# Scores of a two-head attention as one float32 product of raw queries and keys, in place of three float32r products of their parts

## The chip, the cores and the metric

The kernel runs on one core of a Trainium2 chip. The metric is the device time of one execution in microseconds (us); the time of a kernel is the median of its runs.

## What is computed

The change is in the first of three stages. For 4 batches and 8 heads, with 576 positions and 64 values per head, all float32:

```
scores = 1/sqrt(D) * q @ k.T, causal, softmax -> a
local  = a @ v
phi(x) = where(x > 0, x, exp(x) - 1) + 1
mem    = (phi(q) @ M_prev) / (phi(q) . z_prev + 1e-6)
attn   = g * mem + (1 - g) * local          with g = sigmoid(beta)
x      = attn, heads side by side           (2304 tokens x 512)
x      = (h - tanh(h)) @ w_out              with h = x @ w_in        (512 -> 2048 -> 512)
out    = rational(h2) @ w2_out              with h2 = x @ w2_in      (512 -> 2048 -> 512)
```

## The kernel before

**Attention.** Heads are taken in pairs: 16 pairs n, both heads of one side by side on the 128 partitions, 64 rows each. A pair has five units i (`units`, `NU` = 5). Units 0 to 3 are 128 queries against 128, 256, 384 and 512 keys, one matmul group per head; unit 4 takes the last 64 queries of both heads together, with queries of the other head as zeros, against 512 keys and then the last 64.

The work is a pipeline over steps s, one unit entering per step (`step`, L576, with `ORDER` and `LAGS`): scores at once; the exponentials (`numer`) a step later; `scale` two steps later on GpSimd (POOL); `transposes` at lag 3, copied from PSUM by ScalarE (L491, L502); `values` at lag 4; `leave`, VectorE's copy out of PSUM (L818), at lag 5. While the first four pairs run, `values` has one PSUM bank, so the matmuls of a pair's last unit (L535) wait for VectorE's copy of the first four (L818).

**Parts.** `high` (L345) casts q and k to float32r (L351, ScalarE) and `low` (L355) subtracts that from the raw values (L361, VectorE for q, POOL for k), so each is the sum of two float32r parts, q1 + q2 and k1 + k2. `scores` (L413) then makes three products for each head into the same bank, q1 k1 + q1 k2 + q2 k1 (L432 to L438), and VectorE reduces them with the mask (L444).

**phi.** `phi1` to `phi3` (L366, L370, L374), `norm1` on POOL (L380, a product of phi and z), `norm2` on VectorE (L389 reduces that product), `norm3` on POOL (L397). `phiT` (L401) transposes on TensorE (L407), and VectorE copies both results (L410); `memory` (L509) multiplies them with M_prev in float32.

**Order.** The list `prep` (L304) says at which step, relative to the pair's first, each of these is issued, and `late` (L556) shifts some for the first two pairs. `load_k(n)` and `load_q(n)` issue five transfers for pair n + 1 on SyncE's (SP's) queue, at five and four steps before pair n's first unit, since pair n's casts have then been issued; the same queue carries the other inputs, weight loads (`wraw`) and stores (`wk`). Each step also advances a background (`tick`, L249): weights of the MoE are decoded (L164 on ScalarE, L166 to L174 on VectorE) and split (L184 on ScalarE, L186 on POOL), from step 10 on. When the first batch is done, at step 24, the first MoE's items for finished tokens are mixed in (`fill`, L913; L630 and L677 on TensorE), two items in a pair.

**After attention** come the rest of the first MoE and the second one, bound to TensorE and VectorE; none of their code is touched.

Of the kernel before, what the change touches and what calls it, by code (L numbers as in the profile page):

```python
# [9 lines left out]
F32 = mybir.dt.float32  # L10
F32R = mybir.dt.float32r
# [3 lines left out]
ALU = mybir.AluOpType  # L15
# [3 lines left out]
P = 128  # L19
# [41 lines left out]
def kernel(  # L61
# [21 lines left out]
    nc = tc.nc  # L83
    B, NP, _, _, S = qd.shape
# [14 lines left out]
    class Banks:  # L99
        def __init__(self, ids):  # L100
            self.ids, self.n = ids, 0
# [55 lines left out]
    def w_decode(layer, f, s):  # L157


        words = wraw.pop((layer, f, s)).bitcast(U32).rearrange("p (c t) -> p c t", t=2)  # L160
        low, high = words[:, :, 0], words[:, :, 1]
        x = bg.buf("wf", [P, DM], U32, f"wf{layer}_{f}_{s}")
        xf = x.bitcast(F32)
        nc.scalar.activation(xf, high.bitcast(F32), AF.Abs)  # L164
        yield
        nc.vector.tensor_scalar(xf, xf, E_MIN, E_MAX, ALU.max, ALU.min)  # L166
        nc.vector.tensor_scalar(
            x, x, 5, 2, ALU.logical_shift_left, ALU.logical_shift_right
        )
        yield  # L170
        nc.vector.scalar_tensor_tensor(
            x, high, 0xC0000000, x, ALU.bitwise_and, ALU.bitwise_or
        )
        nc.vector.scalar_tensor_tensor(  # L174
            x, low, 29, x, ALU.logical_shift_right, ALU.bitwise_or
        )
        yield
        return xf
# [113 lines left out]
    class Attention:  # L292
# [4 lines left out]
        def __init__(self, x_put, cp, sp, bS, bT, bV):  # L297
            self.x_put, self.cp, self.sp, self.bS, self.bT, self.bV = x_put, cp, sp, bS, bT, bV
            self.NU = NQ + 1
            self.units = [(n, i) for n in range(B * NP) for i in range(self.NU)]  # L300
            self.pair = [{} for _ in range(B * NP)]
            self.u = {}
            self.done = 0
            self.prep = [  # L304
                (-5, self.high, "k"), (-5, self.load_k, None), (-4, self.low, "k"),
                (-4, self.high, "q"), (-4, self.load_q, None), (-3, self.low, "q"),
                (-1, self.phi1, None), (0, self.phi2, None), (1, self.phi3, None),
                (2, self.norm1, None), (2, self.norm2, None), (3, self.norm3, None),
            ]
# [31 lines left out]
        def load_v(self, n):  # L341
            self.load("vn", n, [P, NQ + 1, P], vn, 2)


        def high(self, n, c, eng=None):  # L345

            d = self.pair[n]
            src = d["r" + c]
            d[c + "1"] = self.sp.tile([P, src.shape[1]], F32R, tag=c + "1", name=f"{c}1_{n}")
            if eng is None:  # L350
                nc.scalar.copy(d[c + "1"], src)  # L351
            else:
                eng.tensor_copy(d[c + "1"], src)

        def low(self, n, c, eng=None):  # L355

            d = self.pair[n]
            src = d["r" + c]
            d[c + "2"] = self.sp.tile([P, src.shape[1]], F32R, tag=c + "2", name=f"{c}2_{n}")
            eng = eng or (nc.gpsimd if c == "k" else nc.vector)  # L360
            eng.tensor_tensor(d[c + "2"], src, d[c + "1"].bitcast(F32), ALU.subtract)  # L361

        def phi1(self, n, _):
            d = self.pair[n]
# [36 lines left out]
        def phiT(self, n):  # L401
            d = self.pair[n]
            t = d["phiT"] = self.sp.tile([P, S], F32, tag="phiT", name=f"phiT{n}")
            for j0, j1, w in ((0, NQ, TB), (NQ, NQ + 1, TAIL)):
                ps = self.bT(f"php{n}_{j0}")
                for j in range(j0, j1):
                    nc.tensor.transpose(  # L407
                        ps[:, (j - j0) * P:(j - j0 + 1) * P], d["phi"][:, j, :], self.cp["ident"]
                    )
                nc.vector.tensor_copy(t[:, j0 * P:j0 * P + w], ps[:, 0:w])  # L410


        def scores(self, n, i):  # L413


            d, cp = self.pair[n], self.cp
            u = n * self.NU + i
            sm = cp["sm"][u % len(cp["sm"])]
            pts = []
            if i < NQ:  # L420
                w = (i + 1) * P
                jobs = [
                    (e, 0, w, slice(e * D, (e + 1) * D), cp["mask"][:, TB - i * P:TB + P])
                    for e in range(2)
                ]
                c0 = (i + 1) * P
            else:
                every = slice(0, P)
                jobs = [(0, 0, TB, every, cp["mask"][:, 0:TB]), (1, TB, S, every, cp["mask4"])]
                c0 = 0  # L430
            ps = [self.bS(f"s{n}_{i}_{c}") for c in range(2)]
            parts = (("q1", "k1"), ("q1", "k2"), ("q2", "k1"))  # L432
            for j, (q, k) in enumerate(parts):
                for c, k0, k1, r, _ in jobs:
                    nc.tensor.matmul(  # L435
                        ps[c][:, 0:k1 - k0], d[q][r, c0:c0 + P], d[k][r, k0:k1],
                        start=(j == 0), stop=(j == len(parts) - 1),
                    )  # L438
            for c, k0, k1, _, mask in jobs:
                if i < NQ or c == 0:  # L440
                    pts.append(self.sp.tile(
                        [P, k1 if i < NQ else S], F32, tag=f"p{i}_{c}", name=f"p{n}_{i}_{c}", bufs=1
                    ))
                nc.vector.tensor_tensor_reduce(  # L444
                    out=pts[-1][:, k0:k1], in0=ps[c][:, 0:k1 - k0], in1=mask, scale=-0.125,
                    scalar=3.0e38, op0=ALU.add, op1=ALU.min, accum_out=sm[:, 4 + c:5 + c],
                )
            if i == NQ:
                nc.vector.tensor_tensor(sm[:, 4:5], sm[:, 4:5], sm[:, 5:6], ALU.min)
            self.u[n, i] = {"p": pts, "sm": sm}  # L450
# [105 lines left out]
        def late(self, m, f, r):  # L556

            if m == 0:
                return r + (f in (self.phi3, self.norm1, self.norm2, self.norm3))
            return r + (m == 1 and r < 0 and f not in (self.load_q, self.load_k, self.phi1))  # L560

        def start(self, setup, setup2):

            self.load_k(-1)
            setup()
            self.load_n(0)
            self.high(0, "k")
            self.high(0, "q", nc.vector)
            self.low(0, "q")
            self.low(0, "k")  # L570
            self.load_k(0)
            self.load_q(0)
            setup2()
            self.phi1(0, None)

# [264 lines left out]
    def setup():  # L840
        for t in cp["rq"]:
            nc.vector.memset(t[0:D, TAIL:P], 0.0)
            nc.vector.memset(t[D:P, 0:TAIL], 0.0)
        attn.load_q(-1)
        nc.sync.dma_start(cp["g"], beta.partition_broadcast(P))
        nc.gpsimd.memset(cp["mask"], 0.0)
        nc.gpsimd.affine_select(
            out=cp["mask"][:, TB:TB + P], in_=cp["mask"][:, TB:TB + P],
            compare_op=ALU.is_ge, fill=NEG, base=0, pattern=[[-1, P]],
            channel_multiplier=1,  # L850
        )
        make_identity(nc, cp["ident"])
        for e in range(2):
            r = slice(e * TAIL, (e + 1) * TAIL)
            nc.vector.tensor_copy(cp["mask4"][r], cp["mask"][0:TAIL, TB:TB + TAIL])
        for sm in cp["sm"]:
            nc.vector.memset(sm, 1e-9)
        for pz in cp["pz"]:
            nc.vector.memset(pz[:, :, :, D:D + 1], 1e-6)

    def setup2():
        g, omg = cp["g"], cp["omg"]
        nc.scalar.activation(g, g, AF.Exp, scale=-1.0)
        nc.vector.tensor_scalar(g, g, 1.0, None, ALU.add)
        nc.vector.reciprocal(g, g)
        nc.vector.tensor_scalar(omg, g, -1.0, 1.0, ALU.mult, ALU.add)
        o2 = omg.rearrange("r (p e) -> r p e", e=2)
        for e in range(2):
            r = slice(e * TAIL, (e + 1) * TAIL)
            nc.vector.tensor_copy(cp["omg4"][r], o2[r, :, e])  # L870
# [112 lines left out]
    for s in range(ni + 2):  # L983
        if s < ni:
            t, f = items[s]
# [110 lines left out]
```

## Time and profile before

| | us |
|---|---|
| three runs | 1072.7, 1073.43, 1076.6 (median 1073.43) |
| the profiled execution, its own time | 1075.69 |
| its span, first to last instruction | 1073.9 |
| mean granted TensorE clock | 0.983 |
| busy: TensorE matmul / weight load | 1035.9 / 923.4 |
| busy: VectorE (DVE) / ScalarE (ACT) / GpSimd (POOL) | 876.2 / 689.7 / 439.8 |

Durations are taken from the profiled execution. TensorE's matmuls are pipelined: a record's duration holds its latency, and the distance of starts tells the cost of one in a sequence. Below, a line such as `PE pw L535` is an engine, the tile that is written and the line of the kernel. A wait in brackets is the engine's idle time before the instruction and what ended it.

### The profile page before, as it was taken

How to read it: one execution, taken by the hardware profiler on the slowest of the kernel's cores; microseconds unless marked ns; L12 is line 12 of the kernel's file. 1: busy time of each engine (PE TensorE's matmuls, PEld its weight loads, DVE VectorE, ACT ScalarE, POOL GpSimd, SP SyncE). 2: the span in 40 equal slices, each digit the busy share in tenths (PEclk: the TensorE clock that was granted, in tenths of full speed). 3: DMA queues.
4: the chain of work that ended last, by engine and by line, in shares of the span. 5: the costliest groups of instructions: out<-in, count | busy, mean ns of one | idle time of the engine just before them, and what ended most of it. 6: DMA issues, size and time to landing. Idle time of an engine off the chain costs nothing.

```text
span 1073.9 us, 18786 instructions
## 1 busy us (share of the span) xinstructions
PE 1035.9 (96%) x6704; PEld 923.4 (86%) x6704; DVE 876.2 (82%) x1786; ACT 689.7 (64%) x1507; POOL 439.8 (41%) x407
## 2 busy tenths in 40 slices
PE   6988999999999999999999998989999999999998
PEld 4656778878788999999999998878988989889886
DVE  6899988888767856767675755999999999999997
ACT  5866767768656453333333446878778887787875
POOL 6788877768725210101010103653333423434232
PEclk8987999999999999999999999999999999999999
DMA  5452342424142334444444341100000000000000
GB/s 161 127 163 90 118 133 81 161 81 138 43 130 78 108 108 116 120 127 138 119 118 129 116 137 54 46 1 21 10 1 31 1 20 11 1 30 1 20 11 30
DMA packets 35150, 84.07 MB, mean 78 GB/s; under 512 B 5872, under 2 KB 7920, under 8 KB 35056
## 3 DMA queue, kind: packets, MB, share of 16 engines
q1 hardware_dynamic: 35056, 82.86, 25.1%
q8 instruction: 53, 0.87, 0.3%
q14 instruction: 41, 0.34, 0.1%
HBM read 66.59 MB, written 16.25 MB: 77 GB/s over the span
## 4 chain that ended last, share of the span: by engine, by line
PE 56%; DVE 29%; ACT 8%; issue 4%; DMA 1%; SPq 1%; POOL 0%; POOLq 0%; ACTq 0%; DVEq 0%
PE h L630 20%; PE y L677 17%; DVE vA L741 9%; DVE vA L739 4%; PE s L435 4%; DVE vA L731 4%; PE tp L487 4%; PE y L763 4%; ACT vC L729 4%; ACT vC L730 4%; PE pv L521 3%; DVE vG L737 2%; DVE g L737 2%; PE pw L535 1%; DVE p L444 1%
## 5 line engine op out<-in xcount | busy, mean ns | idle before, releaser
L630 PE MATMUL h<-xs,w 128*128 128x384 f32 (+1 forms) x2448 | 440.1, 328 | 8.9 <-DVE g L745 3.2
L630 PEld LDWEIGHTS h<-xs,w 128*128 128x128 f32 x2448 | 408.1, 189 | 22.7 <-POOL xs L622 4.8
L677 PE MATMUL y<-gh,w 128*128 128x384 f32 (+1 forms) x864 | 216.5, 318 | 0.2 <-ACT gh L665 0.2
L763 PE MATMUL y<-w,gh 128*128 128x512 f32 x576 | 180.8, 395 | 0.2 <-ACT gh L750 0.2
L677 PEld LDWEIGHTS y<-gh,w 128*128 128x128 f32 x864 | 151.6, 188 | 1.3 <-ACT gh L665 0.6
L471 POOL TENSOR_SCALAR p<-p,sm,omg 128x128 f32<-128x128 f32 (+2 forms) x144 | 129.2, 904 | 53.8 <-DVE sm L465 20.1
L622 POOL TENSOR_TENSOR xs<-x,xs 128x256 fp32r<-128x256 f32 (+1 forms) x56 | 49.1, 899 | 232.3 <-ACT xs L621 224.8
L677 PE MATMUL y<-gl,w 128*128 128x384 f32 (+1 forms) x432 | 137.2, 318 | 1.2 <-DVE gl L666 0.9
L659 ACT ACTIVATE g<-h 128x384 f32<-128x384 f32 (+1 forms) x108 | 49.5, 458 | 118.4 <-PE h L630 117.5
L660 DVE TENSOR_TENSOR g<-h,g 128x384 f32<-128x384 f32 (+1 forms) x108 | 55.0, 510 | 86.2 <-ACT g L659 86.1
L763 PEld LDWEIGHTS y<-w,gh 128*128 128x128 f32 x576 | 106.6, 188 | 19.7 <-ACT o L771 1.7
L741 DVE TENSOR_TENSOR vA<-vA,vC 128x384 f32<-128x384 f32 x96 | 120.5, 1255 | 0.0
L763 PE MATMUL y<-w,gl 128*128 128x512 f32 x288 | 114.3, 397 | 1.0 <-POOL gl L752 1.0
L752 POOL TENSOR_TENSOR gl<-g,gh 128x384 fp32r<-128x384 f32 x48 | 57.9, 1207 | 136.7 <-ACT gh L750 114.8
L729 ACT ACTIVATE vC<-vA,coef 128x384 f32<-128x384 f32 x96 | 59.2, 617 | 78.5 <-DVE vA L741 78.5
L752 POOL TENSOR_TENSOR gl<-vG,gh 128x384 fp32r<-128x384 f32 x47 | 58.5, 1245 | 118.1 <-ACT gh L750 101.7
L491 ACT COPY pT<-tp 128x512 f32<-128x512 f32 (+2 forms) x112 | 55.6, 524 | 65.4 <-PE tp L487 64.8
L457 ACT ACTIVATE p<-p,sm 128x128 f32<-128x128 f32 (+2 forms) x144 | 83.5, 587 | 14.9 <-DVE sm L444 8.2
L665 ACT CAST gh<-g 128x384 fp32r<-128x384 f32 (+1 forms) x108 | 51.8, 480 | 57.5 <-PE y L677 56.4
L666 DVE TENSOR_TENSOR gl<-g,gh 128x384 fp32r<-128x384 f32 (+1 forms) x108 | 62.7, 581 | 27.5 <-ACT gh L665 27.5
L677 PEld LDWEIGHTS y<-gl,w 128*128 128x128 f32 x432 | 81.1, 188 | 2.1 <-DVE gl L666 2.1
L435 PE MATMUL s<-k,q 64*128 64x128 f32 (+4 forms) x480 | 72.9, 369 | 9.1 <-ACT k L351 6.5
(96 smaller groups left out, 1745.4 us busy)
## 6 DMA issues: line engine op xcount, KB each, us to landing
wraw<-in_w_in_dram SPq DMA_DIRECT2D x32, 512.0 KB, 4.1
wraw<-in_w_out_dram SPq DMA_DIRECT2D x32, 512.0 KB, 4.0
wk<-wf SPq DMA_DIRECT2D x44, 256.0 KB, 4.4
wx<-wk SPq DMA_DIRECT2D x22, 512.0 KB, 3.3
qn<-in_qn_dram SPq DMA_DIRECT2D x16, 320.0 KB, 4.0
vn<-in_vn_dram SPq DMA_DIRECT2D x16, 320.0 KB, 5.4
rk<-in_kd_dram SPq DMA_DIRECT2D x32, 144.0 KB, 5.2
out_dram<-o SPq DMA_DIRECT2D x18, 256.0 KB, 2.0
```

The lines of the kernel that those rows point to most:

```text
L435: nc.tensor.matmul(ps[c][:, 0:k1 - k0], d[q][r, c0:c0 + P], d[k][r, k0:k1], start=(j == 0), stop=(j == len(parts) - 1),)
L457: nc.scalar.activation(pt, pt, AF.Exp, bias=sm[:, 4 + e:5 + e], scale=-1.0, accum_out=sm[:, 2 * e:2 * e + 1],)
L471: nc.gpsimd.tensor_scalar(pt, pt, v["sm"][:, 6 + e:7 + e], og[:, c:c + 1], ALU.mult, ALU.mult)
L491: nc.scalar.copy(t[:, 0:w, :].rearrange("r t c -> r (t c)"), ps[:, 0:w * P])
L630: nc.tensor.matmul(ps[:, 0:T], wi_of(layer, f, wp, k), xs[k][:, xp], start=(n == 0), stop=(n == 3 * NK - 1),)
L660: nc.vector.tensor_tensor(v["g"], v["h"], v["g"], ALU.subtract)
L666: self.lo.tensor_tensor(v["gl"], v["g"], v["gh"].bitcast(F32), ALU.subtract)
L677: nc.tensor.matmul(ps, wo_of(1, f, w)[:, m * P:(m + 1) * P], v[g], start=(first and j == 0 and m % n == 0), stop=(last and j == 2), skip_g ...
L729: nc.scalar.activation(C, A, AF.Ln, bias=qeps_s, scale=TWO_M60)
L741: nc.vector.tensor_tensor(n["A"], n["A"], n["C"], ALU.mult)
L752: eng.tensor_tensor(o["gl"], o["G"], o["gh"].bitcast(F32), ALU.subtract)
L763: nc.tensor.matmul(acc_of[t][m], g[:, c], wo_of(2, f, w), start=(first and j == 0), stop=(last and j == 2),)
```

## The change

The parts are gone: no `high`, no `low`. `scores` issues for each head one product of the raw float32 tiles; for units 0 to 3 the two heads' products follow each other on different rows of the array, 64 rows each, in two PSUM banks. The loads of the next pair's q and k are issued at the pair's first unit, without the special cases in `late` and `start`. The two copies of phi's transposes go from VectorE to ScalarE.

```diff
             self.prep = [
-                (-5, self.high, "k"), (-5, self.load_k, None), (-4, self.low, "k"),
-                (-4, self.high, "q"), (-4, self.load_q, None), (-3, self.low, "q"),
+                (0, self.load_k, None), (0, self.load_q, None),
                 (-1, self.phi1, None), (0, self.phi2, None), (1, self.phi3, None),
...
-        def high(self, n, c, eng=None):
...
-        def low(self, n, c, eng=None):
...
-                nc.vector.tensor_copy(t[:, j0 * P:j0 * P + w], ps[:, 0:w])
+                nc.scalar.copy(t[:, j0 * P:j0 * P + w], ps[:, 0:w])
...
-            parts = (("q1", "k1"), ("q1", "k2"), ("q2", "k1"))
-            for j, (q, k) in enumerate(parts):
-                for c, k0, k1, r, _ in jobs:
-                    nc.tensor.matmul(
-                        ps[c][:, 0:k1 - k0], d[q][r, c0:c0 + P], d[k][r, k0:k1],
-                        start=(j == 0), stop=(j == len(parts) - 1),
-                    )
+            for c, k0, k1, r, _ in jobs:
+                nc.tensor.matmul(
+                    ps[c][:, 0:k1 - k0], d["rq"][r, c0:c0 + P], d["rk"][r, k0:k1],
+                    start=True, stop=True,
+                )
...
-            return r + (m == 1 and r < 0 and f not in (self.load_q, self.load_k, self.phi1))
+            return r
...
             self.load_n(0)
-            self.high(0, "k")
-            self.high(0, "q", nc.vector)
-            self.low(0, "q")
-            self.low(0, "k")
-            self.load_k(0)
-            self.load_q(0)
             setup2()
```

## Rows read from the trace of the kernel before

**Rows 1.** Stages: stretch, length, busy time of PE, PEld, DVE, ACT, POOL, clock, DMA.

```profile
0.00:32.09 32.09, 21.44 (x133) 14.51 (x134) 22.25 (x82) 17.49 (x47) 20.80 (x28) 0.84 0.49 145
32.09:45.13 13.04, 12.79 (x131) 9.16 (x132) 10.55 (x42) 11.04 (x31) 10.89 (x13) 1.00 0.65 200
45.13:62.23 17.10, 13.19 (x132) 9.18 (x132) 16.69 (x50) 12.79 (x34) 14.58 (x14) 0.95 0.46 142
62.23:81.74 19.51, 16.47 (x132) 12.17 (x132) 17.76 (x50) 12.81 (x33) 15.70 (x15) 0.76 0.41 124
81.74:103.30 21.56, 19.10 (x144) 13.88 (x144) 19.46 (x50) 14.30 (x38) 18.63 (x19) 0.78 0.37 112
103.30:124.36 21.06, 20.44 (x180) 16.49 (x180) 19.38 (x54) 13.46 (x35) 16.83 (x16) 0.92 0.36 116
124.36:301.67 177.31, 175.24 (x1706) 139.44 (x1705) 143.10 (x464) 126.27 (x351) 129.19 (x133) 1.00 0.32 102
301.67:1074.00 772.33, 757.20 (x4152) 708.55 (x4152) 627.01 (x1001) 481.52 (x939) 213.20 (x175) 1.00 0.21 63
```

**Rows 2.** Chain of waits, 235 to 262 us: start, length, engine, tile, line.

```profile
236.49 1.15 PE s L435 x6
...
239.88 0.48 PE s L435 x6
...
243.71 0.55 PE s L435 x6
...
246.08 0.72 PE s L435 x6
...
251.76 1.01 PE pv L509 x4
252.77 0.89 PE s L435 x6
...
255.02 1.15 PE s L435 x6
```

**Rows 3.** Timeline of VectorE, 29 to 71 us: start, length, instruction, idle before it.

```profile
29.32 0.83 DVE L361 TENSOR_TENSOR q<-rq,q 128x640 fp32r<-128x640 f32 x1
...
58.93 1.36 DVE L361 TENSOR_TENSOR q<-rq,q 128x640 fp32r<-128x640 f32 x1
60.21 0.82 DVE L389 TENSOR_REDUCE nrm<-pz 128x10 f32<-128x650 f32 x1
...
70.75 0.82 DVE L410 COPY phiT<-php 128x512 f32<-128x512 f32 x2 [0.66 <-PE php L407]
```

**Rows 4.** Timelines of POOL and of TensorE, 52 to 63 us.

```profile
52.70 1.58 POOL L361 TENSOR_TENSOR k<-rk,k 128x576 fp32r<-128x576 f32 x1
...
58.05 1.55 POOL L380 TENSOR_TENSOR pz<-phi,mz 128x640 f32<-128x640 f32 x1
...
62.23 1.53 PE L535 MATMUL pw<-pT,vn 128*64 128x64 f32 x20 [3.47 <-DVE x L818]
```

**Rows 5.** Stages, L361 alone: stretch, length, busy time of DVE, of POOL, clock.

```profile
62.23:81.74 19.51, 1.36 (x1) 1.43 (x1) 0.76 0.41 124
81.74:103.30 21.56, 1.80 (x1) 1.99 (x1) 0.78 0.37 112
```

**Rows 6.** Stages, L351 alone: stretch, length, busy time of ACT, clock.

```profile
45.13:62.23 17.10, 1.44 (x2) 0.95 0.46 142
```

**Rows 7.** Groups by shape, 32 to 302 us: instruction, count, busy, mean ns, idle.

```profile
L491 ACT COPY pT<-tp 128x512 f32<-128x512 f32 x60 | 33.6, 586 | 18.9 <-PE tp L487 18.9
...
L502 ACT COPY pT<-tq 128x64 f32<-128x64 f32 x15 | 3.3, 221 | 0.0
```

**Rows 8.** DMA issues of the whole span: tile, queue, count, size, us to landing.

```profile
rk<-in_kd_dram SPq DMA_DIRECT2D x32, 144.0 KB, 5.2
```

**Rows 9.** Timeline of ScalarE, 0 to 9 us.

```profile
4.42 1.28 ACT L351 ACT_TABLE_LOAD   x1 [4.42 <-DMA rk<-in_kd_dram]
...
7.21 0.21 ACT L863 ACTIVATE gg<-gg 128x8 f32<-128x8 f32 x1 [0.83 <-DMA gg<-in_beta_dram]
```

More of the change, by code (lines that the diff above doesn't have):

```diff
@@ L342, in load_v @@
             self.load("vn", n, [P, NQ + 1, P], vn, 2)
-        def high(self, n, c, eng=None):
[L347 to L353, printed above, removed]
-        def low(self, n, c, eng=None):
[L357 to L361, printed above, removed]
         def phi1(self, n, _):
```

## The prediction

> **What bounds the kernel now.** I read the stage table first: it cuts the span at the matmuls of L535, which close a pair of heads (the last unit's values). The reader sees three regimes [rows 1]. Up to 124.36 us a pair takes 13.0 to 21.6 us and VectorE is the fullest engine of most stretches: 16.69 of 17.10 us, 17.76 of 19.51, 19.46 of 21.56. From 124.36 to 301.67 TensorE is busy 175.24 of 177.31 us. After that come the two MoEs, which the change does not touch; I carry those 772.33 us over unchanged.
>
> Then the chain of waits in the middle regime: every link is TensorE, one after another, and the same unit of two successive pairs starts at 236.49 and at 255.02, so a pair costs 18.53 us of TensorE [rows 2]. The five score groups of one pair, in order of units 0 to 4, are 0.48, 0.55, 0.72, 0.89 and 1.15 us, 3.79 together. Here the change is paid for.
>
> Last the timelines of the first regime. Just before L535 VectorE does q's low part (58.93), the reduction of norm2 (60.21) and the copy that L535 waits for, while TensorE stands 3.47 us; POOL's product for that reduction starts only at 58.05, behind its own subtract at 52.70 [rows 3, 4]. The granted clock's mean is 0.76 and 0.78 in the fourth and fifth pairs against 1.00 in the second [rows 1]: mixtures of full clock (2.4 GHz) and half (1.2 GHz), in stretches that begin after such idle. Here the change earns.
>
> **Scores on TensorE.** Removed: three float32r products for each head; added: one float32 product. Of a float32 product this trace has L509 (two heads side by side, 512 columns): the program writes two per pair, the trace holds four records, so each product is two passes. The group takes 1.01 us [rows 2]. At 2.4 GHz two passes over 512 columns are 0.43 us at one cycle per column and 0.85 at two; I read it as two, which leaves 0.16 us of start and drain and the heads at the same time. By that, units 0 to 3 (128, 256, 384, 512 columns) cost 0.37, 0.59, 0.80, 1.01. Unit 4 is not split by rows: 576 columns, 0.96 us of passes plus 0.3 of the 0.43 that it now spends beyond its streaming, 1.26. Sum 4.03 against 3.79; the scores' weights are 128 columns wide where L509's are 64, so I take +0.30 per pair. Ends: +0.1 (no more overhead than L509) and +0.8 (all 1.47 us of today's overhead stays on top of 3.09 us of passes); I stay by L509, the same type and column count. The middle regime holds about 9.2 pairs of scores (177.31 / 18.53, less the last units' drain): **+2.8 us**, ends +1 and +7.
>
> **The parts.** Per pair this removes VectorE's q subtract (1.36 in the third and fourth pairs, 1.80 in the fifth), POOL's k subtract (1.43 to 1.99) and ScalarE's two casts (1.44) [rows 3 to 6]. Only the first two lie before something that ends late.
>
> **phi's copies.** VectorE loses 0.82 us per pair and the wait of 0.66 for the transposes in front of it [rows 3]. ScalarE takes two copies from PSUM, priced by its own copies of 512 and 64 columns: 0.59 + 0.22 = 0.81 [rows 7]. It lost 1.44, and is busy 12.8 of 17.1 or more [rows 1], so I cost this at nothing. The new wait on the transposes stands on ScalarE; queued behind it are phi2's exp, a weight cast and the next unit's exp, all used a step or more later. If that cover were gone it would cost 0.66 plus 0.81 per pair.
>
> **Loads.** The same five transfers per pair, issued five steps later for k and four for q, so past the inputs, weight loads and stores of a whole pair on SP. The casts stood five steps behind the transfers, the scores now do: 13 us or more, against a landing of 5.2 us [rows 1, 8]. Nothing. The buffer's last reader is now a score group of the step before; what queues behind that wait of SP's is the step's weight loads, used a tick later or more. For the second pair three other transfers go in front at the start, with 13 us to spare.
>
> **Sum over stretches** [rows 1]. *Start to 32.09:* the q subtract of the second pair goes, and the first scores need no parts. Against it, ScalarE's table load (1.28) stood until k landed at 4.42; its first work will be the gate's exp of L863, released at 7.21 [rows 9], and VectorE's next work hangs on that. From -2.5 to +0.5; I take -1.0. *Second pair (13.04):* TensorE 12.79 busy, so 0. *Third (17.10):* 1.36 + 0.82, and 0.4 for POOL's subtract being gone: VectorE's own took 0.83 at 29.32 and 1.36 at 58.93 beside a POOL instruction [rows 3, 4], so POOL's 1.58 may hold up another one by about that 0.53; ends 0 and 0.8. Less 0.3 for scores: -2.3 (-1.3 to -3.0). *Fourth (19.51):* 1.36 + 0.82 + 0.66 + 0.4: -3.2 (-1.5 to -4.1; VectorE's 16.3 covers the dearer scores). *Fifth (21.56):* the same with 1.80 for the subtract: -3.7 (-2 to -4.8). *Sixth (21.06):* down to the TensorE floor of 18.53 + 0.30, a little above for clock: -2.0 (0 to -2.3). Together -12.2; with +2.8 the net is **-9.4 us**. Other floors: TensorE at full clock needs 13.3 us for an unfilled pair, POOL 14.58 - 1.58 = 13.0 in the third, so VectorE's 14.5 still ends last. The profiled execution is 1075.69 us (span 1073.9), which gives 1066.3; it lies 2.3 us above the median 1073.43, so the forecast is 1064.0.
>
> **A rule weighed.** q's subtract took 0.83 at 29.32, and 1.36 at 58.93, where it ended 0.68 after POOL's product of 58.05 did (59.60) [rows 3, 4]. The Trainium skill (SBUF — State Buffer, Who interferes with whom) says that a VectorE instruction with two SBUF inputs and a GpSimd one that reads SBUF exclude each other for the whole instruction, the later one waiting; the two durations agree. By that rule 0.68 of the 1.36 is POOL's time, not the subtract's, and the sum over three stretches would be about 2 us smaller.
>
> **Rivals.** *(B) The reduction waits for POOL instead.* It reads the product that ends at 59.60, so without q's subtract it starts 0.61 earlier, not 1.36, unless POOL moves up. For it: that POOL item queues behind scales that need VectorE's and ScalarE's results. Against: POOL itself loses 1.58 just before. Then 0.61 + 0.82 in each of three stretches, -4.3; the clock still falls, so -1.2 in the sixth; start 0, scores +4: -1.5, 1072. *(C) The heads do not run side by side in float32 at 64 rows by 128 columns.* No row has this shape in this type; L509 splits columns as well. For against: float32r does it here, a 512-column group of six taking 0.89 [rows 2]. Price: the second head's passes, 2.13 us per pair, in series. Middle regime 9.2 x 2.4 = +22, second pair +2.4, sixth 0, the rest half of its gain, -5.5: +19, **1092**. It turns the sign once the extra exceeds about 1 us per pair. *(D) The clock stays full* as the 3.47 us idle shrinks, and the port relief is whole: most of the low ends, -15.5, with scores at +1: 1059. *(E) The change does not do what it says* and runs one float32r product each: some 2 us less per pair, -18 beside -12: 1043.
>
> **Chances.** A measurement here tells 0.5% (5.4 us) from no change. Forecast 0.54 (1060 to 1068), D 0.11, B 0.23, C 0.10, E 0.02. Faster 0.54 + 0.11 + 0.02 = 0.67; same 0.23; slower 0.10. The range leaves out C, E and the edge of D: 1058 to 1074.5.
>
> **What would show it.** Right: L361, L351 and L410 on VectorE gone, 320 records on the score line where there are 480, score groups in the middle regime of about 0.37, 0.6, 0.8, 1.0 and 1.25, a pair there of 18.8, and the matmuls of L535 of the sixth pair near 112 us instead of 124.36. Wrong: a 512-column group near 1.9 us (C); VectorE idle before the norm2 reduction with POOL as releaser (B); a pair of the middle regime above 19.3, or ScalarE busy without pause around phi's copies with TensorE waiting for them.

## The result, and the profile after

The kernel after takes 1063.97 us (median of four runs, 1061.86 to 1066.53), the kernel before 1073.74 (four runs): a ratio of 0.9907, 95% interval 0.9881 to 0.9934. The forecast was 1064.0. The profiled execution took 1061.86 us with a span of 1060.1.

The stage table of the kernel after, cut as before at the first matmul that closes a pair (now L514), with the same columns; its seven lines answer to the first seven of [rows 1]:

```profile
0.00:28.02 28.02, 19.49 (x116) 11.27 (x116) 16.52 (x76) 15.13 (x44) 15.55 (x25) 1.00 0.50 145
28.02:41.37 13.35, 13.22 (x122) 8.26 (x121) 8.94 (x39) 10.41 (x30) 8.82 (x11) 1.00 0.59 196
41.37:56.34 14.97, 13.32 (x123) 8.32 (x122) 13.90 (x47) 12.48 (x34) 11.77 (x12) 1.00 0.51 159
56.34:71.82 15.48, 13.36 (x122) 8.32 (x122) 14.42 (x47) 12.21 (x33) 13.80 (x14) 1.00 0.54 153
71.82:89.93 18.11, 16.57 (x134) 10.48 (x134) 15.46 (x47) 13.51 (x38) 16.48 (x18) 0.91 0.46 138
89.93:108.76 18.83, 18.83 (x169) 13.96 (x169) 16.87 (x51) 12.78 (x36) 13.53 (x14) 1.00 0.43 128
108.76:288.63 179.87, 178.08 (x1614) 131.02 (x1613) 123.09 (x436) 123.53 (x355) 110.06 (x126) 1.00 0.34 104
```

The score products are 320 records where there were 480, and the casts and subtracts of [rows 5, 6] are gone (L351 and L361 are other lines now); the page's group of the score line:

```profile
L414 PE MATMUL s<-rk,rq 64*128 64x128 f32 (+5 forms) x320 | 76.9, 496 | 6.9 <-DMA rq<-in_qd_dram 4.8
```

The gain lies where the forecast put it, in the first six stretches (124.36 us before, 108.76 after), and the middle regime pays 2.56 us back. The clock's mean is 0.91 in one of these stretches and full in the others; before, it was under 1.00 in five of six.

The chain of waits of the kernel after over one pair of the middle regime answers to [rows 2] (start, length, engine, tile, line):

```profile
221.71 0.88 PE pw L514 x20
...
222.71 1.22 PE s L414 x4
...
226.15 0.42 PE s L414 x4
...
229.91 0.63 PE s L414 x4
...
232.38 0.85 PE s L414 x4
...
239.09 1.06 PE s L414 x4
...
240.52 0.88 PE pw L514 x20
```

Units 0 to 4 take 0.42, 0.63, 0.85, 1.06 and 1.22 us, 4.18 together, where the forecast had 0.37, 0.59, 0.80, 1.01 and 1.26 and the kernel before 3.79. The pair costs 240.52 - 221.71 = 18.81 us against 18.53: 0.28 more, though the groups grew by 0.39. Of the rest, 0.09 is one MoE group, which took 1.69 us in the pair shown before and takes 1.60 here.

Last, the place just before a pair's closing matmuls, on the timelines of VectorE, TensorE and POOL in the third stretch; these answer to [rows 3, 4]:

```profile
54.31 0.83 DVE L370 TENSOR_REDUCE nrm<-pz 128x10 f32<-128x650 f32 x1 [0.66 <-POOL pz L361]
...
55.51 0.68 DVE L791 COPY x<-pv 128x512 f32<-128x512 f32 x1
```

```profile
56.34 0.89 PE L514 MATMUL pw<-pT,vn 128*64 128x64 f32 x18 [1.28 <-DVE x L791]
```

```profile
48.93 1.44 POOL L186 TENSOR_TENSOR w<-wf,w 128x512 fp32r<-128x512 f32 x1
50.39 2.35 POOL L450 TENSOR_SCALAR p<-p,sm,omg 128x128 f32<-128x128 f32 x2
52.72 1.56 POOL L361 TENSOR_TENSOR pz<-phi,mz 128x640 f32<-128x640 f32 x1
```

TensorE's idle before the closing matmuls fell from 3.47 to 1.28 us. Before the reduction of norm2 (now L370) VectorE stands idle for 0.66 us and waits for POOL's product: the wait that rival B named. But the product itself starts 52.72 - 41.37 = 11.35 us after the stretch begins, and 58.05 - 45.13 = 12.92 before [rows 4]: it moved up by 1.57, about the 1.58 of the k subtract that stood in POOL's queue. Up to that subtract POOL's queue runs alike in both: its third item, a scale, starts 6.77 us into the stretch after and 6.79 before.

### The profile page after: what moved, and what is told of

Read it like the earlier page. It is cut to its first block, busy times and chain, and to the rows that moved or that the text cites. A ratio compares the mean times of both kernels' runs of the same rounds, so it can differ in the third digit from the quotient of the medians.

```text
span 1060.1 us, 18385 instructions
## 1 busy us (share of the span) xinstructions
PE 1030.1 (97%) x6544; PEld 902.1 (85%) x6544; DVE 835.8 (79%) x1737; ACT 683.4 (64%) x1508; POOL 403.1 (38%) x391
## 4 chain that ended last, share of the span: by engine, by line
PE 84%; DVE 8%; ACT 3%; issue 2%; POOL 2%; DMA 0%; SPq 0%; POOLq 0%; ACTq 0%; DVEq 0%
PE h L603 33%; PE y L650 18%; PE y L736 16%; PE s L414 5%; PE tp L466 4%; PE pv L500 4%; DVE vA L714 1%; PE pw L514 1%; PE pv L488 1%; DVE vA L704 1%; DVE vA L712 1%; PE php L388 1%; POOL pz L361 1%; DVE gl L639 1%; POOL p L450 1%
## 5 line engine op out<-in xcount | busy, mean ns | idle before, releaser
L450 POOL TENSOR_SCALAR p<-p,sm,omg 128x128 f32<-128x128 f32 (+2 forms) x144 | 115.7, 811 | 75.3 <-ACT p L436 25.5
L714 DVE TENSOR_TENSOR vA<-vA,vC 128x384 f32<-128x384 f32 x96 | 117.3, 1222 | 0.0
L423 DVE CUSTOM_DVE_ANT_0 p<-s,mask 128x512 f32<-128x512 f32 (+4 forms) x160 | 70.3, 476 | 22.5 <-PE s L414 22.4
L414 PE MATMUL s<-rk,rq 64*128 64x128 f32 (+5 forms) x320 | 76.9, 496 | 6.9 <-DMA rq<-in_qd_dram 4.8
```

Source lines behind the costliest of these rows:

```text
L414: nc.tensor.matmul(ps[c][:, 0:k1 - k0], d["rq"][r, c0:c0 + P], d["rk"][r, k0:k1], start=True, stop=True,)
L423: nc.vector.tensor_tensor_reduce(out=pts[-1][:, k0:k1], in0=ps[c][:, 0:k1 - k0], in1=mask, scale=-0.125, scalar=3.0e38, op0=ALU.add, op1=A ...
L450: nc.gpsimd.tensor_scalar(pt, pt, v["sm"][:, 6 + e:7 + e], og[:, c:c + 1], ALU.mult, ALU.mult)
L714: nc.vector.tensor_tensor(n["A"], n["A"], n["C"], ALU.mult)
```

## The experiments

Twelve runs. Each ratio is to runs of the kernel before on the same chip (medians there 1074.5 to 1075.2). A time against the kernel after is the difference of the ratios, times 1074.5, with 0.9894 for the kernel after, from its second measurement; with its first, 0.9907, each would be 1.4 us smaller. The ratios come from all runs of both kernels, so they are not quite those of the medians.

| run | median us | ratio, 95% interval |
|---|---|---|
| e1 raw products, parts kept | 1075.90 | 1.0009, 1.0000 to 1.0017 |
| e2 before, phi's copies on ScalarE | 1074.72 | 1.0004, 0.9995 to 1.0012 |
| e3 after, phi's copies on VectorE | 1065.98 | 0.9915, 0.9902 to 0.9927 |
| e4 parts from the seventh pair on | 1067.23 | 0.9923, 0.9910 to 0.9936 |
| e5 after again | 1062.39 | 0.9894, 0.9876 to 0.9911 |
| e6 after, q's parts kept | 1069.63 | 0.9951, 0.9937 to 0.9964 |
| e7 after, k's parts kept, late | 1074.43 | 0.9992, 0.9981 to 1.0003 |
| e8 heads in series | 1088.59 | 1.0132, 1.0115 to 1.0149 |
| e9 k's parts kept in place | 1072.73 | 0.9977, 0.9964 to 0.9990 |
| e10 norm2 later | 1086.04 | 1.0099, 1.0080 to 1.0117 |
| e11 parts from the eighth pair on | 1067.30 | 0.9931, 0.9916 to 0.9946 |
| e12 two banks for values | 1063.64 | 0.9887, 0.9869 to 0.9905 |

The stretches of the profiled runs, cut at the same matmuls (us; "middle" is the seventh line of the stage table, "rest" the MoEs). A profiled run can lie some 2 us off its kernel's median (before and e1 above it, the kernel after below it); that of e5 agrees with the kernel after within 0.1 us in each of the first seven columns.

| | start | 2nd | 3rd | 4th | 5th | 6th | middle | rest |
|---|---|---|---|---|---|---|---|---|
| before | 32.09 | 13.04 | 17.10 | 19.51 | 21.56 | 21.06 | 177.31 | 772.2 |
| after | 28.02 | 13.35 | 14.97 | 15.48 | 18.11 | 18.83 | 179.87 | 771.5 |
| e1 | 33.12 | 13.08 | 17.08 | 18.37 | 20.46 | 21.50 | 180.09 | 772.7 |
| e2 | 32.45 | 13.53 | 16.87 | 18.21 | 20.38 | 21.44 | 177.30 | 772.6 |
| e3 | 28.29 | 13.33 | 16.24 | 16.79 | 18.05 | 19.16 | 180.20 | 771.0 |
| e4 | 30.89 | 13.36 | 14.96 | 15.48 | 19.58 | 18.54 | 180.62 | 772.2 |
| e6 | 30.58 | 13.09 | 17.05 | 16.17 | 19.61 | 19.14 | 179.88 | 772.3 |
| e7 | 31.47 | 13.77 | 18.06 | 18.14 | 19.47 | 19.72 | 179.85 | 772.9 |
| e9 | 32.27 | 13.09 | 16.27 | 17.53 | 20.36 | 19.16 | 180.07 | 772.1 |
| e10 | 28.05 | 14.51 | 16.82 | 15.54 | 18.92 | 20.00 | 199.43 | 771.4 |
| e11 | 28.11 | 13.36 | 15.89 | 15.51 | 18.21 | 20.49 | 180.60 | 772.1 |
| e12 | 28.41 | 13.35 | 13.76 | 16.60 | 19.80 | 18.81 | 179.92 | 772.5 |

### The three parts of the change, one by one

**e1.** The kernel before, with

```diff
-            parts = (("q1", "k1"), ("q1", "k2"), ("q2", "k1"))
...
+                    ps[c][:, 0:k1 - k0], d["rq"][r, c0:c0 + P], d["rk"][r, k0:k1],
+                    start=True, stop=True,
```

> The kernel before with the score products of the kernel after (one float32 product of the raw tiles per head), while the parts are still cast and subtracted as before and phi's copies stay on VectorE (a third raw buffer for q and k keeps the loads where they were; the parts are left unread). Theory (the gain is VectorE's and POOL's relief in the first six pairs, the score products only cost): the first six stretches keep their sum of 124.4 us within 3 us, a pair of the middle regime goes from 18.53 to 18.8 us, and the time is about 3 us above the kernel before, 1075 to 1079. Rival (the shorter score groups and the missing wait for the parts are what shortens the first stretches): the first six stretches lose more than half of the 15.6 us that the kernel after loses there, and the time is 1070 or less.

The theory held. The first six stretches sum to 123.61 us against 124.36, a pair of the middle regime takes 18.81, and the time is 0.09% above the kernel before, 1.0 us where the theory had about 3. Shorter score groups by themselves bring nothing in the first pairs, so the gain is the parts', the copies' or that of the loads' new place. Nor is it the clock as such: twice a stretch's length times what its mean clock lacks to 1 gives the time at half clock, some 34 us in the six stretches of the kernel before and some 20 in e1 (means of 0.90, 1.00, 0.96, 0.85, 0.92 and 0.92), yet e1 gained 0.75 us there, its dearer score groups included.

**e2.** The kernel before, with

```diff
-                nc.vector.tensor_copy(t[:, j0 * P:j0 * P + w], ps[:, 0:w])
+                nc.scalar.copy(t[:, j0 * P:j0 * P + w], ps[:, 0:w])
```

> The kernel before with phi's copies on ScalarE and nothing else changed. Theory: the third to fifth stretches lose 0.8 to 1.5 us each and the sixth some, 3 to 5 us in all, the middle regime nothing: 1069 to 1071. Rival (q's subtract alone holds the matmuls of L535 up, and norm2's reduction then waits for POOL's product instead of for the copy): no stretch changes by more than 0.5 us, 1073 to 1075.

The theory missed; the time is the rival's. The fourth and fifth stretches lose 1.2 to 1.3 us, but so they do in e1 (1.1 each), where phi's copies stay: in both runs their mean clock is 0.85 or more, against 0.76 and 0.78. Start, second and sixth give half of it back, and the medians are equal. VectorE's timeline and TensorE's in the third stretch:

```profile
59.55 1.36 DVE L361 TENSOR_TENSOR q<-rq,q 128x640 fp32r<-128x640 f32 x1
60.83 0.82 DVE L389 TENSOR_REDUCE nrm<-pz 128x10 f32<-128x650 f32 x1
...
62.02 0.68 DVE L818 COPY x<-pv 128x512 f32<-128x512 f32 x1
```

```profile
62.85 1.43 PE L535 MATMUL pw<-pT,vn 128*64 128x64 f32 x18 [3.62 <-DVE x L818]
```

The reduction follows q's subtract without a pause, as before the change, and TensorE still stands 3.62 us. The rival's reason is not what the rows show: the reduction does not wait for POOL here.

**e3.** The same edit the other way, on the kernel after.

> The kernel after with phi's copies back on VectorE and nothing else changed. Theory: the third to fifth stretches grow by 0.8 to 1.5 us each, TensorE stands longer before the last unit's matmuls and the clock falls more often; 3 to 5 us above the kernel after, 1066.5 to 1069. Rival (without the parts VectorE has room for the copies; what holds then is POOL's product): within 1 us of the kernel after, 1063 to 1065.

In the profiles the theory's stretches show: third +1.27, fourth +1.31, sixth +0.33, fifth nothing. The time, 1065.98, lies between theory and rival: 2.3 us above the kernel after by its second measurement and 0.9 by its first, with intervals that overlap. So with the parts gone phi's copies are worth some 1 to 2 us, and with the parts there nothing. The rows of e3's third stretch, which begins at 41.62, show how they come in:

```profile
52.06 2.22 POOL L450 TENSOR_SCALAR p<-p,sm,omg 128x128 f32<-128x128 f32 x2 [1.44 <-PE tq L477]
54.24 1.55 POOL L361 TENSOR_TENSOR pz<-phi,mz 128x640 f32<-128x640 f32 x1
```

A scale of POOL waits 1.44 us for a transpose of TensorE, which here comes behind VectorE's copies of phi, so POOL's product starts 12.62 us into the stretch, 1.27 later than in the kernel after, and the reduction waits for it.

From e1 to e3 the parts go, and with them the loads' old place and the third raw buffer that held it: 1.0009 - 0.9915 = 0.0094, 10.1 us. No run moves the loads alone. In the kernel after TensorE waits for a transfer of q or k once, 4.85 us before its very first scores; nothing else there shows that their place gains or costs. So the parts are the change, as far as the runs can tell.

### Which part: VectorE's subtract or POOL's

**e6** and **e7** are the kernel after with `high` and `low` back, for q or for k, and the loads a step earlier (`late` shifts these by a step for the first pairs):

```diff
-                (0, self.load_k, None), (0, self.load_q, None),
+                (-1, self.load_k, None), (-1, self.load_q, None),
+                (-4, self.high, "q"), (-3, self.low, "q"),
...
```

> The kernel after, with q's parts still made for the pairs from the second on and left unread: the cast on ScalarE four steps ahead, the subtract on VectorE three steps ahead, at the place where the kernel before had it; for this the loads stand one step earlier. Theory (VectorE's subtract was the dearer part of what held the last unit's matmuls up): the third to fifth stretches grow by 1.4 to 1.8 us each over the kernel after, the sixth by up to 2 as the clock falls; 5 to 8 us above the kernel after in all. Rival (norm2's reduction waits for POOL's product anyway): at most 0.6 us per stretch, under 2 us in all.

> The kernel after, with k's parts still made for the pairs from the second on and left unread: the cast on ScalarE four steps ahead, the subtract on POOL three steps ahead, just before norm1's product; loads one step earlier as in the run with q's parts. Theory: norm1's product and with it norm2's reduction come 0.5 to 1.5 us later in the third to fifth stretches; 2 to 4 us above the kernel after, less than with q's parts. Rival (POOL's product ends last at the reduction, so its subtract was the part that mattered): each of these stretches grows by the whole 1.4 to 1.6 us and the run is 5 us or more above the kernel after, more than with q's parts.

e6 is 6.1 us above the kernel after, inside the theory's 5 to 8, though its third to sixth stretches grow by 2.08, 0.69, 1.50 and 0.31, where the theory had 1.4 to 1.8 in each of three, and the start by 2.56. VectorE and POOL in its third stretch, which begins at 43.67:

```profile
57.42 1.36 DVE L361 TENSOR_TENSOR q<-rq,q 128x640 fp32r<-128x640 f32 x1
58.70 0.82 DVE L389 TENSOR_REDUCE nrm<-pz 128x10 f32<-128x650 f32 x1
```

```profile
56.55 1.55 POOL L380 TENSOR_TENSOR pz<-phi,mz 128x640 f32<-128x640 f32 x1
```

The reduction follows the subtract at once and waits for nothing else. e7 is 10.5 us above: the rival's side. Not all of either price need be the parts'. In both runs ScalarE also waits for transfers: 1.9 us (e6) and 1.0 us (e7) in the start for the second pair's q or k, and 3.4 and 4.3 us near the begin of the third stretch for a weight of the MoE (L164). The kernel after has neither wait; that the loads' place makes them is likely but not shown. The timelines of POOL and VectorE in e7:

```profile
58.32 1.41 POOL L361 TENSOR_TENSOR k<-rk,k 128x576 fp32r<-128x576 f32 x1
59.69 1.54 POOL L380 TENSOR_TENSOR pz<-phi,mz 128x640 f32<-128x640 f32 x1
```

```profile
61.27 0.83 DVE L389 TENSOR_REDUCE nrm<-pz 128x10 f32<-128x650 f32 x1 [2.02 <-POOL pz L380]
```

VectorE waits 2.02 us for a product behind the subtract. But the kernel before had that subtract a step earlier, so **e9** puts it there: e1 with phi's copies on ScalarE and q's parts out.

```diff
-                (-4, self.high, "q"), (-4, self.load_q, None), (-3, self.low, "q"),
+                (-4, self.load_q, None),
...
```

> The kernel before with raw score products, phi's copies on ScalarE and q's parts gone; k's parts are still made at the places that the kernel before had (cast five steps ahead, POOL's subtract four steps ahead, a step before norm1's product) and left unread, with a third raw buffer. It stands beside the run in which POOL's subtract was put directly before norm1's product and the whole gain was lost (1074.4). Theory (what counts is the queue of POOL right ahead of that product): a step earlier, a good part of the subtract is made up before the product; 3 to 7 us above the kernel after, 1065.5 to 1069.5. Rival (what counts is POOL's work as such, wherever it stands): as in that run, 1072 to 1075.

It is 8.9 us above the kernel after: the rival again. The start is 4.25 us of the difference of the profiled runs; the clock is half there for some 7 us in e9 and full in the kernel after. POOL and VectorE in e9's third stretch, which begins at 45.36:

```profile
52.92 1.58 POOL L361 TENSOR_TENSOR k<-rk,k 128x576 fp32r<-128x576 f32 x1
54.47 1.85 POOL L186 TENSOR_TENSOR w<-wf,w 128x512 fp32r<-128x512 f32 x1
56.30 1.75 POOL L469 TENSOR_SCALAR p<-p,sm,omg 128x128 f32<-128x128 f32 x2
58.02 1.55 POOL L380 TENSOR_TENSOR pz<-phi,mz 128x640 f32<-128x640 f32 x1
```

```profile
59.60 0.83 DVE L389 TENSOR_REDUCE nrm<-pz 128x10 f32<-128x650 f32 x1 [0.65 <-POOL pz L380]
```

POOL runs from its subtract to the product without a pause, so a step more of room hides nothing: the product starts 12.66 us into the stretch, 1.31 later than in the kernel after.

Undone alone, q's parts cost 6.1 us, k's 8.9 and phi's copies 2.3, each with what hangs on it in its run. That is 17.3 us, where all three together brought 12.4 over e1 (1.0009 - 0.9894). The third stretch shows the same without the clock, which is full there in the kernel after, e3, e6 and e9, and at half in the kernel before and e1 only as TensorE stands before the closing matmuls: undone alone they cost 2.08 (e6, with its waits for transfers), 1.30 and 1.27 us, all three together (e1) 2.11. Where product and reduction start, in us from the stretch's begin:

| third stretch | product | reduction | behind |
|---|---|---|---|
| before | 12.92 | 15.08 | q's subtract |
| e1, all three kept | 12.91 | 15.06 | q's subtract |
| e6, q's parts kept | 12.88 | 15.03 | q's subtract |
| e9, k's parts kept | 12.66 | 14.24 | the product, 0.65 |
| e3, phi's copies kept | 12.62 | 14.21 | the product, 0.65 |
| after | 11.35 | 12.94 | the product, 0.66 |

Two queues meet at the reduction of norm2: VectorE's, which ends with q's subtract, and POOL's, which ends with the product. The two are not independent, since POOL's scales wait for sums and transposes behind VectorE: in e6 the first of them starts 3.03 us into the stretch instead of 1.52, and the product is late though k's subtract is gone. The product comes much earlier only when all three are gone, so each is worth half of the third stretch's gain or more, given the others.

### The price on TensorE

**e8.** The kernel after, with

```diff
-                    (e, 0, w, slice(e * D, (e + 1) * D), cp["mask"]...
+                    (e, 0, w, slice(0, D), cp["mask"]...
```

> The kernel after, with the second head's product of units 0 to 3 taken from the first head's rows, so that the two heads share the same 64 rows of the array (the second head's scores are left out; the second bank gets the first head's). Theory (the two heads' float32 products run at the same time because they stand on different rows): a 512-column group goes from 1.0 to about 1.9 us, a pair of the middle regime gains 2.1 us to 20.9, the time 20 to 28 us above the kernel after, 1084 to 1092. Rival (the records overlap only in the profile's model and the rows do not matter): a pair stays within 0.2 us of 18.8, 1063 to 1066.

As the theory had it: 1088.59 us. The chain of waits of e8 shows units 0 to 3:

```profile
226.09 0.64 PE s L414 x4
...
230.07 1.06 PE s L414 x4
...
232.95 1.48 PE s L414 x4
...
240.34 1.91 PE s L414 x4
```

Each is dearer than in the kernel after, by 0.22, 0.43, 0.63 and 0.85 us, and a pair takes 20.97 instead of 18.81. The two heads do run side by side in float32 when they stand on different rows. The last step is 0.85 us for 512 columns, 1.66 ns per column, four cycles at 2.4 GHz. The Trainium skill (FP8 and Floating Point Precision, TensorE Precision Notes) says that true float32 takes four passes through the array; in time the run agrees, though the trace holds two records for a product, not four.

**e4** gives the middle regime its three products back; **e11** does it one pair later, with k's parts made four steps ahead and q's two (e4 makes both three to two steps ahead) and the loads a step earlier:

```diff
+            if n < N_PARTS:
+                return
...
+            raw = (("rq", "rk"),)
+            three = (("q1", "k1"), ("q1", "k2"), ("q2", "k1"))
+            parts = raw if n < N_PARTS else three
```

> The kernel after for the first six pairs; the other ten take three products of float32r parts again, cast and subtracted two to three steps ahead of the pair. Theory (the middle regime pays 0.28 us per pair for the float32 passes alone): its nine and a half pairs go back to 18.53 us, 2.7 us gained, of which up to 1 us is given back where the parts of the seventh pair load VectorE and POOL in the fifth and sixth stretches: 1 to 3 us below the kernel after, 1061 to 1063 as a median. Rival (the middle regime's extra is not the score products' but phi's copies and the later loads): the pair stays at 18.8 us and the time at 1064 or above.

> The kernel after for the first seven pairs; the other nine take three float32r products again, with the parts spread out more than in the first hybrid (k's four steps ahead, q's two steps ahead, loads one step earlier). There every second pair of the middle regime took 19.0 instead of 18.5 us. Theory (ScalarE's two casts in one step, beside a MoE item, held a copy of pT back): with the casts apart every pair takes 18.5 us, and the run is 2 to 3 us below the kernel after, a median near 1060. Rival (the parts cost the middle regime as much as they save wherever they stand): the pairs alternate again and the run lies at 1062 or above.

Both theories missed: 3.1 and 4.0 us above the kernel after. Every second pair of the middle regime goes back to 18.5 us, and the others take 19.0 (e4) and 19.3 (e11), so the mean (18.7 and 18.9) is about the 18.8 of the kernel after and the middle regime gives nothing back. Of the 5.6 us by which e4's profiled run is longer, 2.87 are the start's, which is the clock's (see below); e11 loses 0.92 us in the third and 1.66 in the sixth stretch. VectorE's and TensorE's timelines in a dear pair of e11:

```profile
170.04 0.42 DVE L661 TENSOR_TENSOR g<-h,g 128x256 f32<-128x256 f32 x1 [0.52 <-ACT g L660]
170.66 1.06 DVE L366 TENSOR_TENSOR q<-rq,q 128x640 fp32r<-128x640 f32 x1 [0.19 <-ACT q L354]
...
172.43 0.22 DVE L819 COPY x<-pw 128x64 f32<-128x64 f32 x1
```

```profile
172.75 0.44 PE L528 MATMUL pv<-pT,vn 128*64 128x128 f32 x4 [0.45 <-ACT pT L498]
```

The row names ScalarE's copy of pT, but that had ended at 172.51. `values` has one PSUM bank in the middle regime too (`BANKS_1`), and TensorE starts 0.10 us after VectorE's copy of the last unit out of it ends (172.65). The same distance stands in a dear pair of e4: the copy ends at 212.08, the values start at 212.18. So q's subtract stands ahead of that copy on VectorE, and VectorE has waited for ScalarE before it. In a cheap pair VectorE does not wait there, and the copy (190.81) comes ahead of the values (191.54). In the kernel before the subtract stands a step earlier, ahead of norm2 (249.63 and 251.29), so the copy of pw at 257.22 has no subtract in front of it. Spreading the casts left q's subtract where it was; moving it was not tried.

### What holds the first pairs now

**e10.** The kernel after, with norm2 and norm3 a step later for all pairs but the first:

```diff
-                (2, self.norm1, None), (2, self.norm2, None), (3, self.norm3, None),
+                (2, self.norm1, None), (3, self.norm2, None), (4, self.norm3, None),
...
```

> The kernel after, with norm2 a step later and norm3 a step later for the pairs from the second on, so that VectorE's copy of the values (which the last unit's matmuls wait for) comes ahead of norm2's reduction and of its wait of 0.66 us for POOL's product. Theory (in the first six pairs of the kernel after that wait is what ends last ahead of those matmuls): TensorE's idle of 1.28, 1.57 and 0.72 us there goes, the third to fifth stretches lose 1 to 1.5 us each, the clock falls more seldom; 2 to 4 us below the kernel after, a median of 1058.5 to 1061. Rival (VectorE's own load, 13.9 us of a stretch of 15.0, is the floor, or the matmuls of phi's transposes then wait for norm3): within 1 us of the kernel after, 1061.5 to 1064.

Both theories missed: 22 us above the kernel after. VectorE's and TensorE's timelines in the third stretch:

```profile
43.90 0.81 DVE L370 TENSOR_REDUCE nrm<-pz 128x10 f32<-128x650 f32 x1
...
45.87 1.36 DVE L167 TENSOR_SCALAR wf<-wf 128x512 uint32<-128x512 uint32 x1
47.16 0.21 DVE L791 COPY x<-pw 128x64 f32<-128x64 f32 x1
```

```profile
47.47 0.44 PE L500 MATMUL pv<-pT,vn 128*64 128x128 f32 x4 [2.18 <-ACT wf L164]
```

The wait for the first copy is gone; norm2 now stands ahead of the second copy out of the one bank (47.16), for which the next pair's first values wait 2.18 us. They start 0.1 us after that copy ends; the releaser that the row names had long been done. In the middle regime too a pair takes 20.0 to 22.1 us instead of 18.8, which makes most of the loss (199.43 us against 179.87). One pair there shows the same order: the reduction at 240.16, the copy out of the bank at 243.11 to 243.32, the next values at 243.42 after 0.78 us of idle. The other pairs were not taken apart.

**e12.** The kernel after, with

```diff
-BANKS_0 = ([0, 1, 4, 6], [2, 5, 7], [3])
+BANKS_0 = ([0, 1, 4], [2, 5, 7], [3, 6])
```

> The kernel after, with two PSUM banks for the values and three for the scores while the first pairs run (one and four before that). Theory (the last unit's matmuls wait only because the one bank must first be copied out by VectorE, behind norm2's reduction): their idle of 1.28, 1.57 and 0.72 us in the third to fifth stretches goes, of which VectorE's own load of 13.9 to 15.5 us leaves some 2 us to be had: 1 to 3 us below the kernel after, 1059.5 to 1061.5. Rival (VectorE is full, so what TensorE gains there it waits elsewhere, or three banks hold the scores up): within 1 us of the kernel after, 1061.5 to 1064.5.

The rival: 0.7 us below the kernel after, with intervals that overlap. The closing matmuls follow without a wait, and the third stretch takes 13.76 us, 1.21 less. The fourth and fifth take 1.12 and 1.69 more, with a fall of the clock in the fourth (mean 0.90). In the fourth a score group waits for VectorE, which empties the banks, and the scores now have one fewer:

```profile
55.52 0.95 PE L514 MATMUL pw<-pT,vn 128*64 128x64 f32 x20
...
60.53 0.48 PE L414 MATMUL s<-rk,rq 64*128 64x128 f32 x2 [1.49 <-DVE sm L423]
```

No version here beats the kernel after by more than its measurement is uncertain.

### The spread of the kernel after

> The kernel after, unchanged. Its four runs lay near 1061.9 twice and near 1066.3 twice. Theory: the two groups are two places at which the granted clock falls to half in the first six pairs; in the run with a fall near 19 us (as in the hybrid, whose first 31 us are the same code) the first stretch takes 30.9 us, without it 28.0, so the runs fall into groups about 3 to 4.5 us apart, and over more runs the median lies between 1063 and 1066.5. Rival: the groups were chance, and the runs spread evenly over some 2 us around 1062 or around 1066.

The groups are real: over ten runs six lie at 1061.5 to 1062.95 and four at 1065.84 to 1066.53. The median of the second six, 1062.39, is below the 1063 that the theory gave. The place of the fall can be seen in e4, whose first stretch is the same code. Its lines of the stage table, and then those of the kernel after:

```profile
19.00:26.00 7.00, 6.40 (x35) 4.54 (x37) 2.27 (x13) 5.08 (x17) 4.51 (x6) 0.51 0.12 32
26.00:30.89 4.89, 4.89 (x38) 2.20 (x36) 3.48 (x11) 1.90 (x6) 2.68 (x4) 1.00 0.07 27
```

```profile
19.00:26.00 7.00, 6.44 (x63) 4.32 (x65) 4.29 (x20) 6.38 (x22) 5.37 (x8) 1.00 0.22 64
26.00:28.02 2.02, 2.02 (x11) 0.51 (x7) 1.48 (x5) 0.36 (x2) 1.79 (x2) 1.00 0.00 0
```

At half clock (1.2 GHz) TensorE issues 35 matmuls in 7 us instead of 63, and the stretch ends 2.87 us later. In both measurements the dearer runs of the kernel after have a mean clock 0.003 to 0.005 lower, which over 1062 us is 6 to 11 us more at half clock, about such a fall. The mean alone does not tell it: the dearer runs of the second measurement have the 0.995 of the cheaper ones of the first, whose profiled run has two falls of 3.4 us in the rest, near 657 and 711 us, at next to no cost (771.5 us against 771.3 in e5, which does not have them). That it is this fall was not seen in a trace of a dear run, since both profiled runs lay in the cheaper group.

## Why the prediction was right, and where its steps were not

**The number.** Forecast 1064.0, measured 1063.97. That they agree so well is luck: the four runs form two pairs near 1061.9 and 1066.3, the median falls between them, where none of ten runs lies within 1 us, and the second measurement gave 1062.39. A gain of about 10 us is what was forecast and what the runs show.

**Scores.** Right. +0.30 per pair forecast, +0.28 measured; +2.8 over the middle regime, +2.56 measured. The groups alone grew by 0.39, where the sum had 0.24 and a margin. Two passes of two cycles per column and the heads side by side, read off L509 [rows 2], gave each group within 0.05 us. Rival C's price, 2.13 per pair and 1092, is what heads in series cost in e8: 2.16 and 1088.6. The second stretch, costed at 0, paid the same +0.31; it is bound by TensorE as well.

**Third to sixth stretches.** Forecast -2.3, -3.2, -3.7 and -2.0; measured -2.13, -4.03, -3.45 and -2.23. The sums are near and their terms are not. Per pair the forecast credited VectorE's subtract with 1.36 to 1.80, phi's copies with 0.82 to 1.48 and POOL's subtract with 0.4, as terms to be added. The step that failed is the 0.4 for POOL, with "so VectorE's 14.5 still ends last", and the adding itself. e2 shows phi's copies worth nothing in the median while the subtracts stand; in the third stretch k's parts put back alone cost 1.30 us, q's alone 2.08, phi's copies alone 1.27, and all three 2.11. POOL's product at the reduction, rival B's mechanism, is what waits last in the kernel after. "Against: POOL itself loses 1.58 just before" was the right objection to B, and should have been a term of the sum. That the terms came to 2.3 in the third stretch, where 2.13 was measured, is in part luck. In the fourth and fifth the clock has a share that no run sets apart: TensorE spent some 9 us of each at half clock before, none and 3.4 us after, and e1 lost 1.1 us in each with VectorE's queue as it was.

**Start.** Forecast -1.0, measured -4.07 in the profiled run, below its low end of -2.5. Of that 2.87 is the clock, full in this run and half for 6.8 us in e4's run of the same code: with the fall, the step is 30.89 - 32.09 = -1.2. The working left out that the clock could stay full there (before, it was at 0.51 and 0.50 between 16 and 24 us). The table load, feared to delay the gate, came to nothing; ScalarE's timeline of the kernel after, beside [rows 9]:

```profile
0.73 1.28 ACT L836 ACT_TABLE_LOAD   x1 [0.73 <-PEq L1053]
7.23 0.21 ACT L836 ACTIVATE gg<-gg 128x8 f32<-128x8 f32 x1 [5.21 <-DMA gg<-in_beta_dram]
```

The load ran at 0.73 and waited for no data; the gate's exp started at 7.23, against 7.21.

**The clock** was set down as falling as before, with a rival D in which it stays full. It lies between: half for 3.4 us in the first six pairs of the profiled run. Its stretches sum to -13.8 where the medians differ by 9.8, because the profiled run of the kernel after is one of the cheaper group, 2.1 us below its median, and that of the kernel before lies 2.0 above its own.

**The rest** was carried over and came out 0.8 us shorter; over the runs above, whose rest has the same code, it goes from 771.0 to 772.9.

**The rule weighed,** that of the Trainium skill (SBUF — State Buffer, Who interferes with whom): by it the third to fifth stretches would have gained 2 us less than forecast. The third, where the clock plays no part, gained 2.13 us, where the forecast had 2.3 and the rule makes it about 1.6. The durations still agree with the rule: in e6 q's subtract takes 1.36 us again beside POOL's product, which ends at 58.10, 0.68 after the subtract began. The overlap was not the limit, because the product itself moved up.

**Loads and phi's copies on ScalarE,** costed at nothing: nothing is seen of them in the kernel after. The pair of the middle regime is 18.81 us with the copies on either engine (e1, e3 and the kernel after). No run moves the loads alone, and in e6 and e7, where they stand a step earlier, transfers are waited for.

## What to carry to other kernels

Where the late instruction reads the results of two engines, take the queue of each back to the stretch's start; terms taken off the two do not add: here phi's copies were worth nothing alone, and each of the three was worth half of a stretch's gain or more once the others were gone. Before costing a cheaper engine's work as mere contention, look whether its queue runs without a pause up to the instruction that is waited for. When a row names a releaser that had long ended, look for another instruction that ended just before, such as the copy out of a bank. Read a float32 product's cost off another float32 product of the same trace, and check with the rows of the array whether two can run side by side.

## What the runs showed that was not expected

- Two float32 products of 64 rows each, on different rows of the array, cost the time of one: 1.06 us for 512 columns, against 1.91 on the same rows. A column costs 1.66 ns.
- The same first stretch of code took 28.02 or 30.89 us, as the granted clock fell near 19 us or not; the runs of one kernel fall into two groups some 4 us apart, and that the one makes the other was not seen.
- ScalarE's table load ran at 0.73 us while its first user, the gate's exp, waited for a transfer until 7.23; in the kernel before the load itself waited for its first user's transfer, to 4.42 [rows 9]. What makes the difference was not tried.
